# Gate and value products of six token tiles as seven block products, in an attention and expert kernel on one Trainium2 core

## The chip, the core and the metric

The kernel runs on one core of one Trainium2 chip. A core has a matrix engine (TensorE, "PE" in the profile, with its weight loads shown apart as "PEld"), and three engines for elementwise work: VectorE ("DVE"), ScalarE ("ACT") and GpSimd ("POOL"). SyncE ("SP") issues most transfers between DRAM and the core's memory SBUF. TensorE writes its sums to PSUM, which has eight banks of 512 fp32 values for each of 128 partitions; DVE and ACT read them there, POOL does not. Each engine works through its own queue in order; waits between engines are semaphores.

The metric is the time on the device in microseconds, the median of several runs. Where a profile is read, it is that of one execution.

## What is computed

Attention over a sliding window of 64 positions, then a normalised gated expert layer on its output:

```python
scores = q @ k.T / sqrt(64), masked to 0 <= i - j < 64        # 8 batches, 8 heads, 576 positions, 64 wide
attn   = softmax(scores) @ v                                  # -> x: 4608 tokens x 512
xn     = x / sqrt(mean(x * x) + 1e-6) * rms_g
g      = xn @ w_gate                                          # 512 x 1536
val    = xn @ w_val                                           # 512 x 1536
out    = (g * sigmoid(g) * val) @ w_out                       # 1536 x 512
```

Inputs and output are fp32. The kernel gets fp32 accuracy out of fp16 matmuls: each operand is split into a high and a low fp16 part, and a product is the sum of three matmuls (high x high, high x low, low x high), all into the same PSUM bank.

## The kernel before

**Tiles and chunks.** The 4608 tokens are worked off in nine tiles of 512 tokens (`t`, 0 to 8). The 1536 hidden columns are six chunks of 256 (`c`, 0 to 5). For a tile, `expert_in(t, c)` (L821) goes over the two halves `i` of a chunk (128 columns) and makes a gate group (`pg`) and a value group (`pv`): 4 slices of the 512 inputs by three matmuls, each 128x128 weights against 512 tokens. A group fills one of three rotating PSUM banks (`ps_mo`). ACT takes the tanh of the gate (L838), DVE makes the silu of it and multiplies by the value (L839, L840), ACT rounds the result to fp16 (L841), and POOL, or DVE in the last chunk, subtracts to get the low part (L842). The hidden values of a chunk stay in `hs[t, c]`, out of six buffers. After the six chunks, `expert_out(t)` (L1018) multiplies by `w_out`: four blocks `k` of 128 tokens by 12 halves of chunks by three matmuls of 512 columns (`po`), then a scaled copy on ACT (L1003) and a store by SP.

**Attention between them.** Attention for batches 2 to 7 is spread over tiles 0 to 6 as "visits" (L618), one per pair of heads. A visit has the scores of pair `n` on TensorE (L386), masks on DVE (L399) and exponentials on ACT (L402), and the values product of pair `n - 2` (L507). Between the two, POOL scales and moves the weights in 16 small instructions (`move`, L371) and DVE transposes them (`turn`, L374). Then come root mean squares (`roots_of_all`, L697) and `normalise` (L726), which scales `x` and splits it into `xn`. A batch has 576 tokens, so one of its two pieces belongs to one tile and the other to the next.

**Order.** A counter of half steps drives all this. `tick()` (L797) advances it, and everything in `plan` that is due is traced: 32 half steps for a tile, 24 in `expert_in` and 8 in `expert_out`. A planner then orders the instructions of each engine by priority (order of writing) and by modelled readiness. From tile 1, chunk 3, on (`ORDERED`), `group()` (L83) pins TensorE's instructions to the written order; the other engines stay with the planner.

**Code that does not run.** `prepare` (L856), `load_sevens`, `product`, `operands`, `combine` and `expert_in_7` (L933) build a tile from seven block products. They apply to tiles from `FIRST7` on, and `FIRST7 = NT` (9), so no tile uses them here.

**Buffers the change touches.** `wt[0..11]` hold gate and value weights (high and low) of the six chunks, `wt[12..17]` those of `w_out`, `wt[18]` and `wt[19]` are spare. `t2k` is a ring of eight buffers of 2 KB per partition, used for tanh results, stores, roots and sums.

## Time and profile before

| | |
|---|---|
| median of 3 runs | 1028.23 us (1027.82 to 1029.15) |
| the profiled execution, first to last instruction | 1027.3 us |
| mean granted TensorE clock | 0.988 |
| data moved by DMA | 66.11 MB |
| tile 1, about | 208 to 321 us |
| tiles 3, 4, 5, 6, about | 421, 525, 629, 733 us to the next |
| tiles 7 and 8 (without visits), about | 837 to 930.6 and 930.6 to 1024 us |

The profile was taken in one execution; its span leaves out what lies around the first and the last instruction, and the median of the runs is 0.9 us above it. The page gives each engine's busy time and its share of the span, then the costliest groups of instructions by line. Views of the trace give the same for any stretch, the waits of one engine for another, and the instructions in order of time. A group's line names the source line, engine, operation, output and inputs with shapes and count, then busy time and the mean in ns of one instruction, then idle time before it and what ended that. Matmuls are pipelined, so the duration of one (0.38 us for 512 columns) is longer than the distance from one start to the next.

### The profile page before, as it was taken

How to read it: one execution, taken by the hardware profiler on the slowest of the kernel's cores; microseconds unless marked ns; L12 is line 12 of the kernel's file. 1: busy time of each engine (PE TensorE's matmuls, PEld its weight loads, DVE VectorE, ACT ScalarE, POOL GpSimd, SP SyncE). 2: the span in 40 equal slices, each digit the busy share in tenths (PEclk: the TensorE clock that was granted, in tenths of full speed). 3: DMA queues.
4: the chain of work that ended last, by engine and by line, in shares of the span. 5: the costliest groups of instructions: out<-in, count | busy, mean ns of one | idle time of the engine just before them, and what ended most of it. 6: DMA issues, size and time to landing. Idle time of an engine off the chain costs nothing.

```text
span 1027.3 us, 16840 instructions
## 1 busy us (share of the span) xinstructions
PE 993.8 (97%) x6455; PEld 497.1 (48%) x6455; DVE 480.2 (47%) x1333; ACT 409.8 (40%) x1066; POOL 483.6 (47%) x634
## 2 busy tenths in 40 slices
PE   7789989999999999999999999999999999999998
PEld 5544544554444445444544454445444444444445
DVE  5688966343474348333843384337532432201220
ACT  5558885254333433344334433343442222212220
POOL 3326633467856576557645764576455022101200
PEclk9989989999999999999999999999999999999999
DMA  8535641221112111211121112111100000000001
GB/s 288 194 108 178 209 150 47 78 69 45 49 57 78 47 48 67 68 47 47 60 75 48 47 57 78 47 48 45 66 2 1 11 31 1 1 23 20 1 1 41
DMA packets 27793, 66.11 MB, mean 64 GB/s; under 512 B 3008, under 2 KB 3264, under 8 KB 27712
## 3 DMA queue, kind: packets, MB, share of 16 engines
q1 hardware_dynamic: 27136, 63.85, 19.1%
q8 instruction: 51, 0.84, 0.3%
q10 hardware_dynamic: 576, 1.18, 0.3%
q14 instruction: 30, 0.25, 0.1%
HBM read 55.58 MB, written 9.44 MB: 63 GB/s over the span
## 4 chain that ended last, share of the span: by engine, by line
PE 89%; ACT 3%; POOL 2%; DVE 2%; DMA 1%; issue 1%; SPq 0%; ACTq 0%; POOLq 0%; DVEq 0%
PE po L790 9%; PE po L791 9%; PE po L792 9%; PE pv L790 9%; PE pv L791 8%; PE pv L792 8%; PE pg L790 8%; PE pg L791 8%; PE pg L792 8%; PE sc L386 4%; PE xp L507 2%; POOL pm L371 2%; PE x L507 2%; PE tr L489 1%; DMA kv<-kv 1%
## 5 line engine op out<-in xcount | busy, mean ns | idle before, releaser
L371 POOL TENSOR_TENSOR pm<-pm,st 32x288 f32<-32x288 f32 (+1 forms) x384 | 252.8, 658 | 117.9 <-DVE st L428 38.9
L842 POOL TENSOR_TENSOR h<-th,h 128x512 f16<-128x512 f32 x90 | 105.5, 1177 | 184.6 <-ACT h L841 176.3
L790 PE MATMUL pv<-xn,wt 128*128 128x512 f16 x432 | 165.1, 382 | 4.4 <-DVE th L839 4.4
L839 DVE SCALAR_TENSOR_TENSOR th<-th,pg 128x512 f32<-128x512 f32 x108 | 73.7, 683 | 203.8 <-ACT th L838 203.6
L790 PE MATMUL pg<-xn,wt 128*128 128x512 f16 x432 | 163.8, 379 | 1.7 <-ACT wt L235 1.7
L791 PE MATMUL pv<-xn,wt 128*128 128x512 f16 x432 | 165.0, 382 | 0.0
L792 PE MATMUL pv<-xn,wt 128*128 128x512 f16 x432 | 164.8, 381 | 0.0
L791 PE MATMUL pg<-xn,wt 128*128 128x512 f16 x432 | 163.9, 379 | 0.0
L792 PE MATMUL pg<-xn,wt 128*128 128x512 f16 x432 | 163.8, 379 | 0.0
L790 PE MATMUL po<-wt,h 128*128 128x512 f16 (+1 forms) x436 | 162.8, 373 | 0.0
L791 PE MATMUL po<-wt,h 128*128 128x512 f16 (+1 forms) x436 | 162.7, 373 | 0.0
L792 PE MATMUL po<-wt,h 128*128 128x512 f16 (+1 forms) x436 | 162.7, 373 | 0.0
L841 ACT CAST h<-th 128x512 f16<-128x512 f32 x105 | 64.8, 617 | 227.5 <-DVE th L840 227.5
L791 PEld LDWEIGHTS <-wt 128*128 128x128 f16 x872 | 85.6, 98 | 104.8 <-issue 6.5
L792 PEld LDWEIGHTS <-wt 128*128 128x128 f16 x872 | 85.6, 98 | 103.3 <-issue 1.7
L790 PEld LDWEIGHTS <-wt 128*128 128x128 f16 x872 | 85.5, 98 | 103.4 <-issue 2.5
L838 ACT ACTIVATE th<-pg,hsc 128x512 f32<-128x512 f32 x108 | 74.0, 686 | 101.4 <-PE pg L792 85.3
L840 DVE SCALAR_TENSOR_TENSOR th<-pv,th 128x512 f32<-128x512 f32 x108 | 74.0, 685 | 71.3 <-PE pv L792 70.7
L402 ACT ACTIVATE pm<-pm,st 128x128 f32<-128x128 f32 (+1 forms) x216 | 83.3, 387 | 32.6 <-DVE st L399 32.4
L748 POOL TENSOR_TENSOR xn<-xb,xn 128x64 f16<-128x64 f32 (+7 forms) x63 | 49.1, 806 | 83.4 <-ACT xn L746 83.0
L1003 ACT ACTIVATE ot<-po,hsc 128x512 f32<-128x512 f32 (+1 forms) x37 | 25.0, 674 | 120.7 <-PE po L792 120.4
L790 PEld LDWEIGHTS <-h 128*128 128x128 f16 x436 | 42.8, 98 | 48.2 <-issue 0.8
(144 smaller groups left out, 1091.8 us busy)
## 6 DMA issues: line engine op xcount, KB each, us to landing
kv<-kv SPq DMA_DIRECT2D x28, 608.0 KB, 4.5
out<-ot SPq DMA_DIRECT2D x35, 256.0 KB, 2.0
q<-q SPq DMA_DIRECT2D x28, 288.0 KB, 2.8
kv<-kv SPq DMA_DIRECT2D x56, 128.0 KB, 4.6
st<-w_gate SPq DMA_DIRECT2D x6, 1024.0 KB, 5.7
st<-w_val SPq DMA_DIRECT2D x6, 1024.0 KB, 5.8
st_o<-w_out SPq DMA_DIRECT2D x6, 1024.0 KB, 5.0
kv<-kv SPq DMA_DIRECT2D x4, 320.0 KB, 6.2
```

Source lines behind the costliest of these rows:

```text
L371: nc.gpsimd.tensor_tensor(m[to, :us, fr], p[fr, :us, to], r, ALU.mult)
L386: nc.tensor.matmul(out.rearrange("p (n c) -> p n c", c=D), lhsT=qt[hd, j * D : (j + 1) * D], rhs=halves[hd, :1, :] if j == 0 else halves[h ...
L402: nc.scalar.activation(part, part, AF.Exp, bias=low, scale=-1.0, accum_out=total)
L748: eng.tensor_tensor(xn[:, 1, kt, o : o + n], x, hi, ALU.subtract)
L790: nc.tensor.matmul(acc, lhsT=lh, rhs=rh, start=first, stop=False)
L791: nc.tensor.matmul(acc, lhsT=lh, rhs=rl, start=False, stop=False)
L792: nc.tensor.matmul(acc, lhsT=ll, rhs=rh, start=False, stop=last)
L838: nc.scalar.activation(th, acc[0], AF.Tanh, scale=th_scale[:, c : c + 1])
L839: nc.vector.scalar_tensor_tensor(th, th, 1.0, acc[0], ALU.add, ALU.mult)
L840: nc.vector.scalar_tensor_tensor(th, acc[1], 2.0**-41, th, ALU.mult, ALU.mult)
L841: (nc.vector.tensor_copy if t < 2 and E('HHE', 'a' * 24)[12 * t + f] == 'v' else nc.scalar.copy)(hh, th)
L842: (nc.vector if t and c == NC - 1 else nc.gpsimd).tensor_tensor(hl, th, hh, ALU.subtract)
```

## The change

Tiles 3 to 8 compute gate and value of a chunk by seven products of blocks half the size. Take the chunk's 512 inputs as two halves, and the tile's 512 tokens as two halves. Combinations of weight blocks and of token blocks are formed once; seven block products and a few sums of them give what eight give directly (a form of Strassen's scheme). Here a weight block is half of the inputs (two slices of 128) by half of the chunk (128 hidden columns), and a token block is half of the inputs by 256 tokens. One product makes gate and value (`i` = 0 and 1, the two halves of one PSUM bank), each by two slices and three matmuls of 128x128 weights against 256 tokens: 12 matmuls.

What it does, part by part:

- **`FIRST7 = 3`.** Tiles 0 to 2 go as before; tiles 3 to 8 go through `all_sevens`.
- **`prepare(c, i)`**, 12 calls, due at half steps 34 to 72 (tile 1 and the start of tile 2; step 32 begins tile 1). Each copies plain blocks of the weights to DRAM by four transfers, adds high and low parts to fp32 on DVE, makes four sums of blocks on DVE, splits them again (two copies on ACT, one subtraction on POOL and one on DVE) and stores two tiles of 256 KB to DRAM.
- **`load_sevens`** reads 1792 KB for each chunk of each such tile from DRAM into four of the twelve weight buffers, three chunks in turn. The first three are asked for in tile 2; each later one after product 4 of the chunk three before.
- **`combine`** replaces the splitting of `xn` for these tiles: per piece of a batch four sums on DVE and seven pairs of copy (ACT) and subtraction (POOL), where there were four pairs.
- **`seventh(t, c, p)`** runs product `p` into a PSUM bank. Products 1, 5 and 6 are copied to SBUF by ACT (`snap`); products 2, 3 and 7 have a copy added by DVE; the products 6, 7, 4 go on in the bank of 1, and 3 in that of 5. `quad` makes a quarter of the chunk's hidden values: tanh of 256 columns on ACT and two steps of 256 columns on DVE.
- **One pool of PSUM banks.** From tile 3 on the seven pools are closed and a single pool of eight banks serves products, visits, roots and outputs.
- **Written order.** `all_sevens` lays a tile out in 66 slots. Product `p` of chunk `c` stands at slot `7c + PLACE[p]`; free slots from 42 on take the output product, one (block, chunk) pair of six matmuls each, and its last two run over into slots 1 and 5 of the next tile. The half steps that drive the visits are spread evenly over the slots.

```diff
-FIRST7 = NT
+FIRST7 = 3
+SLOTS = 66
+PLACE = {1: 0, 5: 2, 2: 3, 6: 4, 3: 6, 7: 8, 4: 12}
-PREP0, PREP1 = 32.2, 55.5
+PREP0, PREP1 = 34.0, 72.0
+    def prepare(c, i):
+        w = wt[2 * c + i].rearrange("p a (k f) -> p a k f", k=NKD)
...
+        for j in range(2):
+            part = out_of[:, at + TT * j : at + TT * (j + 1)].rearrange("p (k f) -> p k f", k=NKD)
+            nc.sync.dma_start(out=part, in_=w[:, j, :, :P])
+            part = out_of[:, at + 2 * TT + HT * j : at + 2 * TT + HT * (j + 1)].rearrange("p (k f) -> p k f", k=2)
+            nc.sync.dma_start(out=part, in_=w[:, j, 2:, P:])
...
+        for d in range(2):
+            rd = r[d].rearrange("p (k f) -> p k f", k=2)
+            nc.vector.tensor_tensor(rd, w[:, 0, 2 * d : 2 * d + 2], w[:, 1, 2 * d : 2 * d + 2], ALU.add)
...
+        nc.vector.scalar_tensor_tensor(a22, a21, -1.0, a22, ALU.mult, ALU.subtract)
+        nc.vector.tensor_tensor(a21, a11, a21, ALU.subtract)
+        nc.vector.tensor_tensor(a11, a11, a22, ALU.add)
+        nc.vector.tensor_tensor(a12, a12, a11, ALU.add)
...
+            nc.scalar.copy(h, src)
+            (nc.vector if d else nc.gpsimd).tensor_tensor(l, src, h, ALU.subtract)
+        for j, x in enumerate((hi, lo)):
+            nc.sync.dma_start(out=out_of[:, 2 * TT * (2 * i + j) : 2 * TT * (2 * i + j + 1)], in_=x)
...
+    def seventh(t, c, p):
+        if p in (1, 2, 5):
+            acc = any_bank(f"a{p}_{t}_{c}")
+        else:
+            acc = kept[c, "w" if p == 3 else "x"]
+        with group():
+            product(t, c, p, acc, p in (1, 2, 5))
+        if p == 1:
+            kept[c, "x"] = acc
+            snap(acc, t, c, 1)
+        elif p == 5:
+            kept[c, "w"] = acc
+            snap(acc, t, c, 5)
+        elif p == 6:
+            snap(acc, t, c, 6)
+        elif p == 2:
+            nc.vector.tensor_tensor(acc, acc, kept.pop((c, 1)), ALU.add)
+            quad(t, c, 0, 0, acc)
+        elif p == 3:
+            nc.vector.tensor_tensor(acc, acc, kept.pop((c, 6)), ALU.add)
+            quad(t, c, 0, 1, acc)
+        elif p == 7:
+            p5 = kept.pop((c, 5))
+            nc.vector.tensor_tensor(p5, acc, p5, ALU.add)
+            quad(t, c, 1, 1, p5)
+        else:
+            quad(t, c, 1, 0, acc)
+            load_sevens(NC * (t - FIRST7) + c + 3)
...
+    for n in range(2 * NC):
+        at_step(PREP0 + (PREP1 - PREP0) * n / (2 * NC), partial(prepare, n // 2, n % 2))
...
+    early.close()
+    shared["banks"] = ctx.enter_context(tc.tile_pool(name="ps_8", bufs=8, space=PSUM))
+    late = ctx.enter_context(tc.tile_pool(name="late", bufs=1))
+    all_sevens()
```

More of the change, by code (lines that the diff above doesn't have):

```diff
@@ L407, in scores_of_pair @@
         sc = [
-            pool.tile([P, TT], F32, tag=tag, name=f"sc_{n}_{h}").rearrange("p (i k) -> p i k", k=P)
+            (any_bank(f"sc_{n}_{h}") if shared else pool.tile([P, TT], F32, tag=tag, name=f"sc_{n}_{h}"))
+            .rearrange("p (i k) -> p i k", k=P)
             for h, (pool, tag) in enumerate(((ps_sc, "sc"), (ps_tr, "tr")))
@@ L898, in load_sevens, with block @@
+    def block(p, i, j):
+        if p in SUMS:
+            return 2 * TT * (2 * i + j) + HT * SUMS[p]
+        at = 8 * TT + 3 * TT * i
+        return at + (2 * TT + HT * j if p == 4 else TT * j + HT * (p - 1))
+    SUMS = {6: 0, 7: 1, 3: 2, 5: 3}
     def load_sevens(r):
@@ new lines, in tile_window_attention_moe, with snap, quad @@
+    kept = {}
+    def snap(src, t, c, p):
+        d = wt[11][:, 1, :].bitcast(F32) if p == 5 else late.tile([P, TT], F32, tag=f"s{p}", name=f"s{p}_{t}_{c}")
+        nc.scalar.copy(d, src)
+        kept[c, p] = d
+    def quad(t, c, i, half, acc):
+        if (c, "th", i) not in kept:
+            kept[c, "th", i] = wk.tile([P, TT], F32, tag="t2k", name=f"th_{t}_{c}_{i}", bufs=T2K), []
+        th, done = kept[c, "th", i]
+        cols = th[:, half * HT : (half + 1) * HT]
+        nc.scalar.activation(cols, acc[:, :HT], AF.Tanh, scale=th_scale[:, c : c + 1])
+        nc.vector.scalar_tensor_tensor(cols, cols, 1.0, acc[:, :HT], ALU.add, ALU.mult)
+        nc.vector.scalar_tensor_tensor(cols, acc[:, HT:], 2.0**-41, cols, ALU.mult, ALU.mult)
+        done.append(half)
+        if len(done) == 2:
+            kept.pop((c, "th", i))
+            hh, hl = hs[t, c][:, 0, i, :], hs[t, c][:, 1, i, :]
+            nc.scalar.copy(hh, th)
+            (nc.vector if c == NC - 1 else nc.gpsimd).tensor_tensor(hl, th, hh, ALU.subtract)
@@ new lines, in all_sevens, with out_unit @@
+    def all_sevens():
+        units = {}
+        outs = []
+        for t in range(FIRST7, NT):
+            base = SLOTS * (t - FIRST7)
+            for c in range(NC):
+                for p, at in PLACE.items():
+                    units[base + (NC + 1) * c + at] = partial(seventh, t, c, p)
+            last = NC - 1
+            order = [(0, c) for c in range(last)] + [(1, c) for c in range(last - 1)] + [(0, last), (1, last - 1), (1, last)]
+            order += [(k, c) for k in range(2, TT // P) for c in range(NC)]
+            outs += [(base + (NC + 1) * last + 7, t, k, c) for k, c in order]
+        pos = {}
+        def out_unit(t, k, c):
+            if t == NT - 1 and k == TT // P - 1:
+                if c == 0:
+                    for e in range(2):
+                        es = slice(e * DM // 2, (e + 1) * DM // 2)
+                        po = any_bank(f"po_{t}_{k}_{e}")[:, es]
+                        for c in range(NC):
+                            chunk_out(po, t, c, k, c == 0, c == NC - 1, es)
+                        store(po, t, k, es)
+                return
+            if c == 0:
+                pos[t, k] = any_bank(f"po_{t}_{k}")
+            po = pos[t, k]
+            chunk_out(po, t, c, k, c == 0, c == NC - 1)
+            if c == NC - 1:
+                store(po, t, k)
+        n = SLOTS * (NT - FIRST7)
+        for slot in range(n):
+            h = half_steps * (FIRST7 - 1) + half_steps * slot / SLOTS
+            while steps["now"] <= half_steps + h:
+                tick()
+            if slot in units:
+                units.pop(slot)()
+            elif outs and slot >= outs[0][0]:
+                out_unit(*outs.pop(0)[1:])
+        assert not units
+        while outs:
+            out_unit(*outs.pop(0)[1:])
@@ L1022, in expert_out @@
                 es = slice(e * DM // halves, (e + 1) * DM // halves)
[L1023 removed]
+                po = ps_mo.tile([P, DM], F32, tag="mo", name=f"po_{t}_{k}_{e}")[:, es]
                 for c in range(NC):
@@ L1119, in tile_window_attention_moe @@
             first_full = 2
[L1120 to L1134 removed]
+    for t in range(first_full, FIRST7):
+        for c in range(NC):
+            in_order["on"] |= (t, c) >= ORDERED
+            expert_in(t, c)
+            if t == FIRST7 - 1 and c % 2:
+                load_sevens(c // 2)
         expert_out(t)
+    early.close()
+    shared["banks"] = ctx.enter_context(tc.tile_pool(name="ps_8", bufs=8, space=PSUM))
+    late = ctx.enter_context(tc.tile_pool(name="late", bufs=1))
+    all_sevens()
     assert not plan
[L1137 removed]
 def kernel(**inputs):
```

150 lines of the change are left out of this document (25 added, 125 removed).

## The prediction

> **What bounds the kernel now.** I read the page first, then a view of busy time by stretches cut at the tile borders, then TensorE's own waits, then the last 25 us instruction by instruction.
>
> ```profile
> span 1027.3 us, 16840 instructions
> PE 993.8 (97%) x6455; PEld 497.1 (48%) x6455; DVE 480.2 (47%) x1333; ACT 409.8 (40%) x1066; POOL 483.6 (47%) x634
> ```
>
> The columns of the second view are length, then busy time and instructions of each engine (PEld is the weight load, beside PE), granted clock and DMA.
>
> ```profile
> core 0: us, PE busy (x) PEld busy (x) DVE busy (x) ACT busy (x) POOL busy (x), PEclk, DMA share, GB/s
> 208.00:321.00 113.00, 108.46 (x829) 54.50 (x828) 58.48 (x188) 48.13 (x162) 75.97 (x104) 1.00 0.20 61
> 421.00:525.00 104.00, 104.00 (x734) 51.51 (x730) 51.18 (x148) 40.57 (x120) 62.91 (x84) 1.00 0.19 56
> 837.00:930.60 93.60, 93.60 (x436) 42.42 (x434) 17.95 (x26) 18.41 (x28) 11.55 (x10) 1.00 0.03 12
> ```
>
> The rows are tile 1, tile 3 and tile 7. In the last two TensorE is busy for the whole stretch at a granted clock of 1.00, and no other engine is busy for two thirds of it. Only tile 1 has holes, 113.0 - 108.5 = 4.5 us. So from tile 2 on the time is the number of matmuls times their pitch, and what leaves TensorE's queue leaves the span, as long as no other engine turns late. A busy TensorE is not one at its peak, so I need the pitch:
>
> ```profile
> 999.66 0.38 PE L790 MATMUL po<-wt,h 128*128 128x512 f16 x1
> ...
> 1015.64 0.38 PE L792 MATMUL po<-wt,h 128*128 128x512 f16 x1
> 1015.85 0.27 PE L790 MATMUL po<-wt,h 128*128 128x256 f16 x1
> 1015.85 0.10 PEld L791 LDWEIGHTS <-h 128*128 128x128 f16 x1
> ...
> 1019.78 0.27 PE L790 MATMUL po<-wt,h 128*128 128x256 f16 x1
> ...
> 1023.60 0.27 PE L792 MATMUL po<-wt,h 128*128 128x256 f16 x1
> ```
>
> 75 matmuls of 512 columns start 15.98 us apart from first to last: 15.98 / 74 = 0.216 us each. Then come 72 of 256 columns, the shape the change uses: 7.75 / 71 = 0.1092 us each, a new weight load with every one. The load (0.10) fits under a 256-column matmul with a hundredth of a microsecond to spare. Tile 7 confirms the pitch: 432 x 0.216 = 93.3 of its 93.6 us.
>
> **The term that goes.** One 256-column chunk of gate and value takes 4 groups x 12 = 48 matmuls of 512 columns now, 10.37 us. After, it is 7 products x 12 = 84 matmuls of 256 columns, 9.17 us. Saved: 1.20 us, times 6 chunks and 6 tiles, **43.1 us**. The output product and the attention stay. A tile with attention would go from 104.0 to 96.8 us.
>
> The code for block products in the kernel before never runs (its first tile is NT), so nothing else is removed. The 252 products each begin with a wait on another engine. At 1019.78 the second half of the columns starts in a new accumulator, and the pitch holds. If each product's start laid one weight load bare, it would cost 252 x 0.10 = 25 us. I take nothing, the nearest row, and keep 25 as the far end.
>
> The Trainium skill's page "TensorE: Matmul & The Clock Gate" (Part 3, The mechanism) speaks against this change: it says that a weight load overlaps running matmuls only when they use different row groups, and here all use the whole array. By that rule every load would be paid beside its matmul. The rows above disagree, 0.1092 us for both together; the price is a rival below.
>
> **What the vector engines get, per chunk.** Rows by shape, mean ns of one:
>
> ```profile
> L838 ACT ACTIVATE th<-pg,hsc 128x512 f32<-128x512 f32 x108 | 74.0, 686 | 101.4 <-PE pg L792 85.3 <-POOL h L842 15.7
> L839 DVE SCALAR_TENSOR_TENSOR th<-th,pg 128x512 f32<-128x512 f32 x108 | 73.7, 683 | 203.8 <-ACT th L838 203.6
> L841 ACT CAST h<-th 128x512 f16<-128x512 f32 x105 | 64.8, 617 | 227.5 <-DVE th L840 227.5
> L842 POOL TENSOR_TENSOR h<-th,h 128x512 f16<-128x512 f32 x90 | 105.5, 1177 | 184.6 <-ACT h L841 176.3 <-DVE h L841 6.0
> L842 DVE TENSOR_TENSOR h<-th,h 128x512 f16<-128x512 f32 x16 | 13.2, 828 | 7.5 <-ACT h L841 7.5
> L492 DVE COPY pt<-tr 128x256 f32<-128x256 f32 x16 | 6.7, 418 | 6.7 <-PE tr L489 6.6
> L694 DVE SCALAR_TENSOR_TENSOR r<-r,r 128x256 f32<-128x256 f32 x6 | 3.5, 582 | 0.2
> L1003 ACT ACTIVATE ot<-po,hsc 128x256 f32<-128x256 f32 x2 | 0.9, 473 | 6.7 <-PE po L792 6.7
> L748 POOL TENSOR_TENSOR xn<-xb,xn 128x256 f16<-128x256 f32 x8 | 5.7, 738 | 5.4 <-ACT xn L746 5.3
> ```
>
> DVE now does 4 x 0.683 = 2.7 us. After: 3 sums with PSUM (512 columns, 0.68 each) and 8 steps of 256 columns, which lie between 0.418 (a 256 copy out of PSUM) and 0.683; I take 0.45: 2.1 + 3.6 = 5.7. ACT: 3 snapshots (nearest 0.617), 4 tanh of 256 (0.473) for 2 of 512 (0.686): 2.4 more. Per tile DVE gets 6 x 3.0 = 18 and ACT 14. The operand sums per batch add some 8 DVE instructions and six more copy-and-subtract pairs on ACT and POOL: 8 x 0.58, 6 x 0.47 and 6 x 0.74, so 5, 3 and 4 us. A tile with attention then has DVE 51 + 18 + 5 = 74, ACT 58 and POOL 67 of 96.8 us. No engine passes TensorE; DVE, at 76%, comes nearest.
>
> **Their slack decides.** Products 1 and 6 share a bank with three products between them: 3 x 12 x 0.1092 = 3.9 us, in which the snapshot (0.6) must be through. The same holds from 6 to 7, from 7's sum to 4, and from 5 to 3. Now three banks rotate, two groups ahead are 5.2 us, tanh and multiply take 1.4: 3.8 left. So 3.3 remain where 3.8 did, with more work ahead in each queue. Elsewhere there is room: product code holds at most four of the eight banks and a visit four; chunk 5's last hidden values take 0.5 + 2 x 0.45 + 0.6 + 0.8 = 2.8 us, and the output product wants them five slots of 1.3 later; the next tile's first operand needs some 9 roots' steps and 4 scalings (13 x 0.58) and a pair (1.2), 9 us, in the 15 slots left at step 25, 20 us.
>
> ```profile
> 523.43 0.27 PE L386 MATMUL x<-kv,q 64*64 64x64 f32 x2
> ...
> 525.76 0.39 PE L790 MATMUL po<-wt,h 128*128 128x512 f16 x1
> 524.08 0.35 ACT L402 ACTIVATE pm<-pm,st 128x64 f32<-128x64 f32 x1 [2.81 <-DVE st L399]
> ...
> 528.71 0.68 ACT L570 ACTIVATE ssq<-xb 128x576 f32<-128x576 f32 x1
> DVE pm L374 <- POOL pm L371: 63.1, 20, 5.4
> ```
>
> An attention visit keeps ACT for 5.3 us (524.08 to 529.39), of which the first 1.7 lie beside its own 2.3 us on TensorE, so a snapshot may come 3 us late: just inside. Worse is DVE standing before the transpose (L374) for POOL's moves: 3.2 us on average, 5.4 at most, and the sums, tanh and snapshots queue behind it. The mean is all of the slack, the longest exceeds it by 2. With 16 visits in tiles 3 to 6 that is 0 to 32 us; I take **4**, since the mean just fits.
>
> **The weight sums (prepare).** Twelve halves at steps 34, 37.2, ... 68.8; ten fall in tile 1 (steps 32 to 63). Each: on DVE two adds and a subtract of 512 columns (0.828) and four sums of 256 (0.582), 4.8 us; on ACT two copies, 1.2; on POOL one subtract, 1.2; on SP six transfers, the last two behind those subtracts. Tile 1 gets DVE 58 + 48 = 106 of 113 us, POOL 76 + 12. It is also the one place where TensorE already waits:
>
> ```profile
> PE pv L790 <- DVE th L839: 1.6, 1, 1.6
> PE x L386 <- DMA kv<-kv: 1.5, 1, 1.5
> PE x L507 <- DVE st L399: 1.4, 1, 1.4
> ```
>
> A half that runs on DVE in one piece (4.8) exceeds the slack of 3.8 by 1.0, twelve times 12 us; broken up by other work it costs nothing. I take **5** and keep 0 to 25, as each half also pushes POOL's moves, behind which values and loads wait.
>
> Two-input DVE work beside POOL is slower, and the sums are of that kind:
>
> ```profile
> 307.47 0.95 DVE L693 TENSOR_TENSOR r<-r 128x192 f32<-128x192 f32 x1
> 310.42 0.36 DVE L693 TENSOR_TENSOR r<-r 128x192 f32<-128x192 f32 x1
> 305.64 4.53 POOL L748 TENSOR_TENSOR xn<-xb,xn 128x384 f16<-128x384 f32 x4 [3.12 <-ACT xn L746]
> ```
>
> The same instruction takes 0.95 while POOL is busy (to 310.17) and 0.36 after. The Trainium skill's page "SBUF — State Buffer" (SBUF: two separate sides) gives the reason as an exclusive lock on a port pair that the two share, held for a whole instruction; the trace agrees. If all seven DVE instructions of a half lost the 0.6 us that these rows show, ten halves would lay 42 us more on DVE in tile 1, about 148 of 113: the heavy rival below.
>
> **New loads.** Each chunk of a product tile reads 1792 KB from DRAM, into buffers free after product 4 of three chunks back: eight products later it is needed, 10.5 us, plus 2.3 if a visit lies between.
>
> ```profile
> kv<-kv SPq DMA_DIRECT2D x28, 608.0 KB, 4.5
> st<-w_gate SPq DMA_DIRECT2D x6, 1024.0 KB, 5.7
> SPq L336 <- POOL ssq L575: 68.2, 13, 11.8
> ```
>
> From 608 KB in 4.5 us to 1024 KB in 5.7 is 1.2 us for 416 KB, so 1792 KB should land in about 7.9 us: hidden by 2.6. Only three chunks of a tile (18 loads) are that tight, the others have the output product between. The pool change at tile 3 I put at **1** (a store's copy and its wait); the tail is the same.
>
> **The sum.** 1027.3 - 43.1 + 4 + 5 + 1 = 994.2 for the profiled span; the median of the runs lies 0.9 above it: **995**.
>
> **Rivals.**
> - *All hidden.* Only the 43.1 counts: 1028.2 - 43 = 985. For: tiles 2 to 8 show no wait now, and the load on each engine stays under 80%. Against: DVE's wait before L374 is as long as the slack. 0.16.
> - *DVE falls behind.* Halves run in one piece or meet POOL (12 to 25 us), and each of 16 visits shows 1 us: 985 + 13 + 16 = 1014; with the port loss in full 1026. For: DVE at 94% in tile 1. Against: no sum has to be early, the last is read in tile 3. 0.24.
> - *Loads late* (the slow side). SP issues in order. The wait of a kv load for POOL's ssq, 68.2 / 13 = 5.2 us, may stand ahead of the weights. If so for all 18, each is late by 7.9 + 5.2 - 10.5 = 2.6 us, 47 us in sum, and with the 10 of the main case 1042. It decides from 1.8 us a load (33 us over 18). Against: kv loads come just after visits, and two of a tile's three tight loads are issued before one. 0.06.
> - *The loads of weights aren't covered*, so the change doesn't save: 84 x (0.109 + 0.10) = 17.6 against 48 x (0.216 + 0.10) = 15.2 per chunk, 36 x 2.4 = 86 us more: 1114. The tail speaks against it. This is the rule of the TensorE page named above. 0.01.
>
> **How the numbers follow.** Main case 988 to 1004 with 0.51; 985 with 0.16; 1004 to 1026 with 0.24; the rest, 0.09, near or above 1028. This kernel's measurement tells about 0.2% (2 us) from no change. Faster 0.91, same 0.02, slower 0.07. The range runs from 985 to 1019: it leaves out the top of the DVE case, the slow ones and the lowest corner.
>
> **What would show it.** In the changed profile: products starting every 0.109 us; tiles 7 and 8 at 86 to 87 us and tiles 3 to 6 at 97 to 99; a tile 1 of 113 to 120 us, with waits of TensorE on DVE; TensorE's waits in tiles 3 to 6 on the snapshots and the sum of product 7, next to visits. The prediction is wrong if the pitch in the products is over 0.115, if products wait on DMA, if tile 1 grows by over 15 us, or if tiles 7 and 8, which have no attention, exceed 90.

## The result, and the profile after

The changed kernel takes 1045.59 us (median of 4 runs, 1044.15 to 1047.58) against 1028.03 us (1027.75 to 1029.15) for the kernel before on the same chip: ratio 1.0168, 95% interval 1.0152 to 1.0184. It is 1.7% slower, where I had put 995 us. (Of the runs below, one of the six executions of e15b took 4795.1 us and is left out of its median.)

```profile
span 1045.8 us, 20545 instructions
...
PE 975.9 (93%) x7751; PEld 632.9 (61%) x7751; DVE 668.9 (64%) x1713; ACT 510.6 (49%) x1303; POOL 543.1 (52%) x679
...
PE 58%; DVE 18%; POOL 12%; ACT 7%; issue 3%; DMA 2%; SPq 0%; POOLq 0%; DVEq 0%; ACTq 0%
```

The last line is from the chain of work that ended last. DVE and POOL hold 30% of it now, 4% in the kernel before; no engine but TensorE looks full, and TensorE itself is down to 93%. The view by stretches, with the columns of the prediction, cut where the first gate matmul or product of tiles 1, 2, 4 and 7 starts:

```profile
211.00:348.20 137.20, 116.52 (x797) 57.02 (x797) 110.84 (x262) 59.37 (x181) 101.67 (x116) 0.93 0.27 90
348.20:459.00 110.80, 106.29 (x725) 52.39 (x724) 66.64 (x165) 44.87 (x131) 74.38 (x95) 0.98 0.37 115
...
561.50:667.80 106.30, 100.87 (x941) 74.33 (x940) 72.96 (x196) 55.22 (x157) 68.43 (x91) 0.97 0.51 162
...
866.90:953.00 86.10, 86.10 (x649) 63.42 (x648) 37.58 (x71) 34.55 (x62) 18.83 (x16) 1.00 0.44 144
```

Tile 7 is where I had put it, and full. Tile 1 is 25 us longer than before, tile 2 7 us, and tile 4, which should be at 97, is at 106. The products themselves, in the order of time (start, duration; a row of "x12" is one product):

```profile
879.98 1.47 PE L922 MATMUL a<-xn,wt 128*128 128x256 f16 x12
881.29 1.47 PE L922 MATMUL a<-wt,wt 128*128 128x256 f16 x12
882.60 4.09 PE L922 MATMUL a<-xn,wt 128*128 128x256 f16 x36
886.53 2.78 PE L922 MATMUL a<-wt,wt 128*128 128x256 f16 x24
889.15 1.04 PE L922 MATMUL a<-xn,wt 128*128 128x256 f16 x8
```

84 matmuls from 879.98 to 889.15: 9.17 us, the chunk I had worked out. So the saving is there, and what eats it is in the waits (us in total, times, longest):

```profile
DVE pm L377 <- POOL pm L374: 48.1, 19, 5.2
...
PE x L511 <- DVE st L402: 34.7, 13, 6.9
...
PE pv L794 <- DVE th L843: 8.9, 5, 3.9
```

L402 is the mask of a visit, L511 its values product. They meet in a bank: the scores of a pair's first block stand in the bank that the values of the pair two visits earlier are written to. The end of tile 3, TensorE and then DVE:

```profile
553.09 0.38 PE L796 MATMUL po<-wt,h 128*128 128x512 f16 x1
557.51 1.53 PE L511 MATMUL x<-pm,kv 64*64 64x64 f32 x20 [4.04 <-DVE st L402]
558.98 0.61 PE L794 MATMUL po<-wt,h 128*128 128x512 f16 x1
...
561.51 0.85 PE L922 MATMUL a<-xn,wt 128*128 128x256 f16 x3
```

```profile
534.27 0.42 DVE L692 TENSOR_SCALAR r<-tot 128x256 f32<-128x256 f32 x1 [0.96 <-PE tot L704]
...
542.58 2.99 DVE L744 SCALAR_TENSOR_TENSOR xb<-xb,gsb,r 128x256 f32<-128x256 f32 x4
545.50 1.23 DVE L377 STREAM_TRANSPOSE pm<-pm 128x1024 f32<-128x1024 f32 x1
...
549.40 0.48 DVE L692 TENSOR_SCALAR r<-tot 128x320 f32<-128x320 f32 x1
...
555.38 1.94 DVE L744 SCALAR_TENSOR_TENSOR xb<-xb,gsb,r 128x320 f32<-128x320 f32 x4
557.23 0.22 DVE L402 CUSTOM_DVE_ANT_0 pm<-x,blocked 128x64 f32<-128x64 f32 x1
```

From 534.3 DVE works without a hole: roots and scaling of one piece, the transpose, the token sums of that piece, then roots and scaling of the second piece (its token sums follow the mask). The mask of the visit, whose scores were done by 551.4, comes at 557.2. After the wait the clock is half: six output matmuls start 2.53 / 6 = 0.42 us apart (558.98 to 561.51), not 0.216. In the kernel before, at the same place of tile 4:

```profile
603.53 0.36 DVE L688 TENSOR_SCALAR r<-tot 128x192 f32<-128x192 f32 x1 [1.14 <-PE tot L700]
...
621.39 2.87 DVE L740 SCALAR_TENSOR_TENSOR xb<-xb,gsb,r 128x384 f32<-128x384 f32 x4
627.75 0.23 DVE L399 CUSTOM_DVE_ANT_0 pm<-x,blocked 128x64 f32<-128x64 f32 x1 [3.50 <-PE x L386]
```

The same unbroken run, 21 us, and then DVE waited 3.5 us for the scores. That was its whole slack. The change takes 9 us from the interval (the last two visits of a tile are 24 us apart, 33 before, since slots share out the half steps evenly) and puts the token sums of the first piece into the run. Between the visit at 526.1 and the next visit's mask at 557.2 DVE is busy for 26.9 us, more than the whole interval.

In tile 1, DVE and then TensorE:

```profile
293.99 1.25 DVE L377 STREAM_TRANSPOSE pm<-pm 128x1024 f32<-128x1024 f32 x1 [5.20 <-POOL pm L374]
...
297.88 1.28 DVE L870 TENSOR_TENSOR r<-wt 128x512 f32<-128x512 f16 x2
299.09 0.21 DVE L402 CUSTOM_DVE_ANT_0 pm<-x,blocked 128x64 f32<-128x64 f32 x1
```

```profile
299.36 1.53 PE L511 MATMUL x<-pm,kv 64*64 64x64 f32 x20 [6.87 <-DVE st L402]
```

DVE stands (waits at the head of its queue) for 5.2 us before the transpose for POOL's moves, then does what has piled up, weight sums (L870) among it, and the mask is 6.9 us late.

### The profile page after: what moved, and what is told of

Its sections match the earlier page's. It is cut to its first block, busy times and chain, and to the rows that moved or that the text cites. A ratio compares the mean times of both kernels' runs of the same rounds, so it can differ in the third digit from the quotient of the medians.

```text
span 1045.8 us, 20545 instructions
## 1 busy us (share of the span) xinstructions
PE 975.9 (93%) x7751; PEld 632.9 (61%) x7751; DVE 668.9 (64%) x1713; ACT 510.6 (49%) x1303; POOL 543.1 (52%) x679
## 4 chain that ended last, share of the span: by engine, by line
PE 58%; DVE 18%; POOL 12%; ACT 7%; issue 3%; DMA 2%; SPq 0%; POOLq 0%; DVEq 0%; ACTq 0%
PE a L922 26%; POOL pm L374 10%; PE po L794 6%; PE po L795 6%; PE po L796 6%; DVE xb L744 3%; PE sc L389 2%; ACT pm L405 2%; DVE r L697 2%; DVE r L698 2%; PE xp L511 2%; DVE r L699 2%; PE x L511 2%; DVE pm L377 1%; PE pv L794 1%
## 5 line engine op out<-in xcount | busy, mean ns | idle before, releaser
L922 PEld LDWEIGHTS <-wt 128*128 128x128 f16 x3024 | 295.8, 98 | 42.9 <-issue 2.2
L922 PE MATMUL a<-xn,wt 128*128 128x256 f16 x1728 | 203.8, 274 | 1.2 <-ACT ot L1041 0.8
L954 POOL TENSOR_TENSOR h<-th,h 128x512 f16<-128x512 f32 x60 | 69.1, 1159 | 154.5 <-ACT h L953 139.3
L922 PE MATMUL a<-wt,wt 128*128 128x256 f16 x1224 | 146.2, 273 | 0.0
L947 DVE SCALAR_TENSOR_TENSOR th<-th,a 128x256 f32<-128x256 f32 x108 | 45.3, 419 | 65.1 <-ACT th L946 65.0
L946 ACT ACTIVATE th<-a,hsc 128x256 f32<-128x256 f32 x108 | 51.3, 475 | 52.6 <-PE a L922 29.8
L796 PEld LDWEIGHTS <-h 128*128 128x128 f16 x436 | 43.1, 99 | 49.4 <-issue 2.2
L794 PEld LDWEIGHTS <-h 128*128 128x128 f16 x436 | 43.3, 99 | 46.9 <-issue 3.0
L795 PEld LDWEIGHTS <-h 128*128 128x128 f16 x436 | 43.1, 99 | 46.0 <-issue 3.4
L794 PE MATMUL pv<-xn,wt 128*128 128x512 f16 x144 | 57.6, 400 | 8.9 <-DVE th L843 8.9
L389 PE MATMUL sc<-kv,q 64*64 64x128 f32 (+1 forms) x1056 | 56.5, 296 | 8.1 <-DMA q<-q 5.1
L777 ACT CAST xn<-xb 128x192 f16<-128x192 f32 (+7 forms) x33 | 12.9, 423 | 101.7 <-DVE xb L744 101.5
L377 DVE STREAM_TRANSPOSE pm<-pm 128x1024 f32<-128x1024 f32 x24 | 29.8, 1243 | 48.1 <-POOL pm L374 48.1
L511 PE MATMUL x<-pm,kv 128*64 128x64 f32 (+1 forms) x480 | 26.1, 250 | 34.7 <-DVE st L402 34.7
```

The source lines that it names most:

```text
L389: nc.tensor.matmul(out.rearrange("p (n c) -> p n c", c=D), lhsT=qt[hd, j * D : (j + 1) * D], rhs=halves[hd, :1, :] if j == 0 else halves[h ...
L511: nc.tensor.matmul(xp[hd, c * D : (c + 1) * D], lhsT=vv[j][rows, hd], rhs=w, start=True, stop=True, skip_group_check=True,)
L794: nc.tensor.matmul(acc, lhsT=lh, rhs=rh, start=first, stop=False)
L795: nc.tensor.matmul(acc, lhsT=lh, rhs=rl, start=False, stop=False)
L796: nc.tensor.matmul(acc, lhsT=ll, rhs=rh, start=False, stop=last)
L922: nc.tensor.matmul(acc[:, i * HT : (i + 1) * HT], lhsT=ws[l][:, kt, :], rhs=b[:, m, kt, :], start=at_start, stop=kt == 1 and j == 2, skip_ ...
```

## The experiments

Theory: the loss is (a) the weight sums in tiles 1 and 2 and (b) the end of tiles 3 to 5, both through DVE's order. Rivals: the transfers, the products' own evacuation, the pool of banks. The table has all runs: median, ratio to the kernel before on the same chip with its interval, and the lengths of tiles 1 to 7 from the trace (first gate matmul or product of a tile to that of the next).

| run | us | ratio | t1 | t2 | t3 | t4 | t5 | t6 | t7 |
|---|---|---|---|---|---|---|---|---|---|
| before | 1028 | 1 | 112.5 | 103.9 | 103.9 | 103.9 | 103.9 | 99.6 | 93.2 |
| after | 1045.6 | 1.0168 | 137.2 | 110.8 | 102.5 | 106.3 | 105.7 | 93.4 | 86.1 |
| e1 | 1052.8 | 1.0233 (1.0218-1.0248) | 133.9 | 106.3 | 103.9 | 103.9 | 103.9 | 99.6 | 93.2 |
| e2 | 1030.4 | 1.0017 (1.0008-1.0026) | 111.9 | 107.6 | 103.8 | 107.2 | 106.5 | 92.9 | 86.1 |
| e3 | 1043.2 | 1.0141 (1.0124-1.0158) | 136.7 | 110.8 | 95.7 | 105.4 | 104.9 | 99.7 | 86.1 |
| e4 | 1055.2 | 1.0257 (1.0241-1.0272) | 136.3 | 110.4 | 106.6 | 109.2 | 109.2 | 92.9 | 86.1 |
| e5 | 1039.9 | 1.0110 (1.0095-1.0125) | 136.7 | 107.5 | 103.2 | 105.0 | 105.4 | 92.9 | 86.1 |
| e6 | 1045.8 | 1.0163 (1.0148-1.0178) | 130.2 | 117.1 | 102.3 | 106.5 | 106.0 | 92.9 | 86.1 |
| e7_from6 | 1037.6 | 1.0080 (1.0065-1.0095) | 114.3 | 109.4 | 108.2 | 111.8 | 112.6 | 90.3 | 86.1 |
| e7_from7 | 1041.8 | 1.0126 (1.0109-1.0143) | 112.6 | 111.4 | 106.1 | 107.3 | 115.4 | 100.6 | 83.5 |
| e8 | 1033.3 | 1.0046 (1.0031-1.0061) | 114.1 | 107.3 | 108.9 | 109.1 | 114.2 | 90.3 | 86.1 |
| e9 | 1052.4 | 1.0224 (1.0209-1.0240) | 143.8 | 109.2 | 107.3 | 100.9 | 103.0 | 97.1 | 86.1 |
| e9_from6 | 1039.2 | 1.0098 (1.0082-1.0115) | 114.1 | 109.0 | 107.3 | 109.0 | 109.9 | 100.1 | 86.1 |
| e10 | 1044.3 | 1.0144 (1.0122-1.0166) | 138.9 | 107.0 | 103.6 | 105.8 | 106.1 | 92.9 | 86.1 |
| e11 | 1007.4 | 0.9787 (0.9771-0.9803) | 107.5 | 103.9 | 103.9 | 103.9 | 106.9 | 90.3 | 86.1 |
| e12 | 1052.0 | 1.0230 (1.0212-1.0247) | 134.4 | 103.9 | 103.9 | 103.9 | 103.9 | 99.6 | 93.2 |
| e13 | 1023.0 | 0.9952 (0.9934-0.9970) | 107.5 | 103.9 | 103.9 | 103.9 | 103.9 | 99.6 | 93.2 |
| e14 | 1003.7 | 0.9762 (0.9742-0.9782) | 108.0 | 103.9 | 103.9 | 104.9 | 99.5 | 92.5 | 86.1 |
| e15b | 1023.6 | 0.9953 (0.9932-0.9973) | 107.3 | 108.6 | 103.5 | 105.8 | 106.1 | 92.9 | 86.1 |
| e15 | 1001.9 | 0.9745 (0.9725-0.9764) | 107.3 | 104.9 | 101.5 | 97.6 | 98.5 | 92.5 | 86.1 |

**e1, sums alone.**

```diff
-FIRST7 = 3
+FIRST7 = NT
```

> All nine tiles as in the kernel before; the twelve halves of weight sums are made and stored, and never read. Theory (the sums are what tile 1 and tile 2 lose, +24.7 and +6.9 us in the changed kernel): 1028 + 31 = about 1059 us, tile 1 near 137 us, tiles 3 to 8 as before. Rival (the sums alone cost what I predicted, 5 us, and tile 1 grew for another reason, for instance the planner's order of what comes later): 1033 us, tile 1 below 120.

24 us, in tile 1 (21.4) and tile 2 (2.4) alone: the theory's side, 7 us short of its 31. Tiles 1 and 3:

```profile
209.80:343.70 133.90, 113.05 (x797) 55.96 (x797) 106.55 (x257) 58.46 (x178) 98.60 (x112) 0.96 0.28 94
...
450.00:554.00 104.00, 104.00 (x726) 51.47 (x725) 51.11 (x145) 40.58 (x120) 62.97 (x85) 1.00 0.19 57
```

**e2, the sums' arithmetic left out.**

```diff
-        r = [wk.tile(...) for d in range(2)]
...
+        for j in range(2):
+            nc.sync.dma_start(out=out_of[:, 2 * TT * (2 * i + j) : 2 * TT * (2 * i + j + 1)], in_=wt[2 * c + i][:, j, :])
```

> The changed kernel without the arithmetic of the weight sums: the transfers that fill the DRAM copy stay, plain weights stand where the sums would be (the output is another). Theory (DVE, ACT and POOL work of the sums holds tile 1 and 2): about 1045.6 - 31 = 1015 us, tile 1 back at 113 and tile 2 at 104, tiles 3 to 5 still at 105. Rival (the transfers and SP's queue do it): above 1035 us, tile 1 still above 130.

Tiles 1 and 2 together are 28.5 us shorter (248.0 to 219.5), so arithmetic and not transfers. The total falls by only 15 us, mostly since tile 0 took 160.4 us and not 151.6: in all three runs without the sums it was 8 to 11 us longer, with a wait of 5 to 6 us of TensorE for a `kv` transfer that the others lack. SP issues that transfer at about the same time (163.6 in e2, 162.3 in the changed kernel), but in e2 the scores that wait for it stand ahead of a value group in TensorE's queue. Why the order differs there isn't known, so those runs are read by tiles. Tile 2 stays 3.7 us longer than before even without the sums, with a wait of 2.5 us for the mask of its last visit.

**e3, a bank of its own for the first block.**

```diff
-            visits[n][0](xp[:, XSPLIT:])
+            visits[n][0](any_bank(f"fi_{n}") if shared else xp[:, XSPLIT:])
```

> The changed kernel, and from tile 3 on the 64 scores of a pair's first block get a PSUM bank of their own, so that the values product of the pair two visits earlier does not share it with them and does not wait for their mask. Theory (the shared bank lays DVE's backlog bare): the waits of 1.2 to 4.7 us at the visits of tiles 3 to 6 go, 18 us, and 5 us of lowered clock behind them: 1045.6 - 23 = about 1023 us. Rival (DVE is late anyway, and what comes next on TensorE, the second half of the values or a product whose bank waits for DVE's sum, waits in its place): within 5 us of 1045.6.

The rival: the values no longer wait, and TensorE does three products later, 3.42 us for a snapshot (L937) that ACT makes behind the exponentials of the late mask. The wait now falls into the next tile (t3 less, t6 more; tiles 3 to 6 sum to 405.7 against 407.9). DVE is late; the bank only says where it shows.

**e4, the old share of the half steps.**

```diff
-            h = half_steps * (FIRST7 - 1) + half_steps * slot / SLOTS
+            tile_no, s = divmod(slot, SLOTS)
+            h = half_steps * (FIRST7 - 1 + tile_no) + (24 * s / 45 if s < 45 else 24 + 8 * (s - 45) / 21)
```

> The changed kernel with the half steps of a tile laid over its 66 slots as they lay in time before: 24 half steps on the first 45 slots, the last 8 on 21 slots (before this run, 8 half steps on 16.5). Normalising, and with it roots, scaling and the sums of token blocks, gets 31 us up to the last visit, as in the kernel before, and not 24. Theory (DVE has too little time at the end of a tile): the waits of 4.0 to 4.7 us at the ends of tiles 3 to 5 go, 13 us and 4 of clock: about 1029 us. Rival (the visits, now 22 us apart in the first part of a tile in place of 24, make DVE wait longer for POOL's moves before the transpose): 1045 us or slower.

Slower, against the theory as I put it. The last visit's scores start at 549.85, 31 us after the visit before:

```profile
551.04 1.94 DVE L744 SCALAR_TENSOR_TENSOR xb<-xb,gsb,r 128x320 f32<-128x320 f32 x4
553.01 0.96 DVE L783 TENSOR_TENSOR t<-xb 128x320 f32<-128x320 f32 x1
...
556.07 0.89 DVE L789 TENSOR_TENSOR t<-xb,t 128x320 f32<-128x320 f32 x1
556.89 0.21 DVE L402 CUSTOM_DVE_ANT_0 pm<-x,blocked 128x64 f32<-128x64 f32 x1
```

The planner set the mask behind the token sums (553.0 to 557.0), and the run had begun 10 us after the visit, not 8. Length of the interval is not the only thing; the order in it counts.

**e5, token sums left out.**

```diff
-        nc.vector.tensor_tensor(t3, x22, x12, ALU.subtract)
...
+        parts("t1", x12)
+        parts("t2", x22)
+        parts("t3", x12)
+        parts("t4", x21)
```

> The changed kernel without the four sums of token blocks on DVE per piece of a batch: the seven pairs of copy and subtraction stay, and work on plain blocks (the output is another). The run e4 gave the last visit of a tile 31 us in place of 24, and its mask still came 7 us late, because the planner had put the four sums ahead of it. Theory (roots, scaling and token sums are one unbroken run of 28 us on DVE, and the mask of the visit stands behind it): 6.4 us less per tile on DVE, so the waits of 4.0 to 4.7 us at the ends of tiles 3 to 5 go, with the lowered clock behind them: tiles 3 to 5 near 98 us, in all about 1027 us. Rival (roots beside POOL's moves are what is too long, 0.75 us where 0.42 would do; the sums only add to it): waits shrink by less than half, 1038 us or more.

The rival: tiles 3 to 5 gained 1 us in all. Roots, scaling and the transpose alone run from 529.0 to 550.3 and overrun a visit at 545.0.

**e6, e7, where the halves stand.**

```diff
-PREP0, PREP1 = 34.0, 72.0
+PREP0, PREP1 = 34.0, 87.0        # e6
+PREP0, PREP1 = 66.0, 183.0       # e7_from6, with FIRST7 = 6
+PREP0, PREP1 = 66.0, 215.0       # e7_from7, with FIRST7 = 7
```

> The changed kernel with the twelve halves of weight sums at half steps 34 to 82.6 in place of 34 to 68.8: seven of them in tile 1 and five in tile 2, where ten and two were. Theory (tile 1 loses because DVE is overfull there, so the loss falls faster than the number of halves): tile 1 near 124 us and tile 2 near 110, in all about 1033 us. Rival (each half costs about 2.5 us wherever it stands): tile 1 near 130, tile 2 near 118, in all about 1045 us.

> Products only in tiles 6, 7 and 8, and the twelve halves of weight sums spread from half step 66 to 173 (tiles 2 to 5, one in 9.75 half steps). Theory (the products gain what was predicted where DVE has room; the sums cost little where DVE is half idle and each has its own 30 us): tile 6 near 93, tiles 7 and 8 near 86 and 89, no wait of over 1 us in tiles 2 to 5: 1028 - 6 - 7 - 4.5 - 0 to + 3 = 1010 to 1014 us. Rival (each half costs 2 to 2.5 us wherever it stands, as it did in the run of sums alone): 1010 + 24 to 30 = 1034 to 1040 us.

> Products only in tiles 7 and 8, which have no attention visits, and the halves of weight sums spread from half step 66 to 203 (tiles 2 to 6, one in 12.4 half steps). Theory: tiles 7 and 8 near 86 and 89 us, nothing else changes: 1028 - 7 - 4.5 + 0 to 3 = 1016 to 1020 us, some 6 us above the kernel with products from tile 6. Rival (each half costs 2 us or more everywhere): 1040 us or more.

Rival in all three. In e6 tile 1 gives 7.0 us and tile 2 takes 6.3: some 2 us a half. In e7 even one half in 40 us lays a wait open, mostly of the values for the mask, and most where it falls between the last two visits (tile 5 of e7_from7: 6.6 us). My picture of a queue that is overfull only in tile 1 fell here.

**e8, halves right behind a visit.**

```diff
-        at_step(PREP0 + (PREP1 - PREP0) * n / (2 * NC), partial(prepare, n // 2, n % 2))
+        at_step(half_steps * (2 + n // 3) + (3.5, 11.5, 19.5)[n % 3], partial(prepare, n // 2, n % 2))
```

> As the kernel with products from tile 6, but each of the twelve halves of weight sums stands 4 half steps after a visit (phases 3.5, 11.5 and 19.5 of tiles 2 to 5), where the halves of the two kernels before laid no gap open; none stands between the last two visits of a tile. Theory (a half costs only where DVE or POOL has less slack to the next visit's mask than the half takes: DVE idles 3.5 us ahead of the last visit of a tile in the kernel before, and POOL's moves leave little in the others): gaps of TensorE in tiles 2 to 5 fall from 24 to under 8 us: 1037.5 - 15 to - 22 = 1016 to 1022 us. Rival (each half costs some 2 us wherever it stands, through POOL's subtraction and the slower DVE beside it): 1032 to 1038 us.

Rival by its time, but now each tile from 2 to 5 shows the same: no wait at its first visit, 0.2 us at the second, 2.7 at the third (0.45 and 3.0 when counted from the start of the last score matmul, as below). POOL's ten moves there in e8, and in the kernel before:

```profile
480.91 8.82 POOL L374 TENSOR_TENSOR pm<-pm,st 32x288 f32<-32x288 f32 x10
```

```profile
474.64 7.05 POOL L371 TENSOR_TENSOR pm<-pm,st 32x288 f32<-32x288 f32 x10
```

And what DVE and TensorE of e8 make of it:

```profile
495.04 1.25 DVE L377 STREAM_TRANSPOSE pm<-pm 128x1024 f32<-128x1024 f32 x1 [5.78 <-POOL pm L374]
```

```profile
499.22 1.39 PE L511 MATMUL x<-pm,kv 64*64 64x64 f32 x20 [2.74 <-DVE st L402]
```

DVE's part of the half was through at 488. But DVE's sums slow POOL's moves beside them, 0.88 us each in place of 0.71, DVE stands for them 5.8 us, and behind the transpose queue gate work and then the mask. In the kernel before the transpose was as close: it started at 463.86 after a stand of 3.74, DVE was free at 466.5, and the values came at 468.0, so with 0.2 for the mask some 1.3 us were left. And it isn't needed then: the order of DVE's instructions has the transpose of pair n, which the visit of pair n + 2 uses, ahead of the mask of pair n + 1. The planner sets it a whole visit early, where it has to stand.

**e9, the second piece after the last visit.**

```diff
-        events = ... + [(n0, partial(normal, 0)), (n1, partial(normal, 1))]
+        events = ... + [(n0, partial(normal, 0))]
+        if FIRST7 <= b < B - 1:
+            events += [(n1, defer)] + [(LATER + 0.8 * k, resume) for k in range(6)]
...
+    x5 = cp.tile([P, 5, S], F32, name="xb")
-... T2K ... = ... 8 ...
+... T2K ... = ... 7 ...
```

> The changed kernel, and at the ends of tiles 3, 4 and 5 the second piece of the batch (needed only a whole tile later) is normalised after the last visit, in five steps from half step 1 to 4.2 of the next tile; only its sum of squares and the first instruction of its roots stay ahead. The five pairs' worth of x stand in one buffer of five slots, so that the next batch's first pair does not overwrite it, and the ring of 2 KB buffers is 7 instead of 8 to make room. Theory (the last visit's mask comes late because 28 us of DVE work stand in 24 us between two visits, 11 of them for this piece): the waits of 4.2 to 4.7 us at the ends of tiles 3 to 5 go, with the lowered clock behind them, tiles 3 to 5 at 97 to 100 us: about 1022 to 1028 us. Rival (the work is late wherever it stands: the next tile's first products, or the mask of its first visit, wait instead): tiles 3 to 5 at 103 us or more, 1040 us or more.

> Both edits together: products from tile 6, halves of weight sums 4 half steps after a visit in tiles 2 to 5, and the second piece of the batch at the end of tile 5 normalised after the last visit. Theory: the wait at the end of tile 5 (4.3 us and the clock behind it, 8 us in all in the kernel with products from tile 6) goes too: 4 to 8 us below the kernel with the phases alone, about 1012 us. Rival: no difference to it within 2 us.

Rival again in the first: the waits at the ends of tiles 3 to 5 shrink to 2 us or nothing, but others come, such as the next tile's second chunk for a snapshot:

```profile
482.97 5.28 PE L959 MATMUL a<-xn,wt 128*128 128x256 f16 x24 [3.62 <-ACT wt L974]
```

Tile 1 also lost 6.6 us, with a wait of 11.0 us for a `kv` transfer. The second, e9_from6, fits neither side: it is 5.8 us slower than e8, since tile 5 gains 4.3 us and tile 6 loses 9.8, with a wait of 4.8 us for a snapshot.

**e10 to e12, the transpose at its written place.**

```diff
-MOVES = (8.7, 7, 4.5, 4)
+MOVES = (4, 7, 4.5, 4)
...
-                events.append((visit_at(n + 2) - half_steps * (b - 1) - 3, partial(turned, hp)))
+                at_visit = visit_at(n + 2) - half_steps * (b - 1)
+                lead = 7.2 if at_visit % half_steps == 31.5 else 3
+                events.append((at_visit - lead, partial(behind, [partial(turned, hp)], (nc.vector,))))
```

> The changed kernel, and the transpose of a pair's weights on DVE is kept at its written place (after all DVE work written before it; 3 half steps ahead of the visit that needs it, 7.2 where that visit is the last of a tile). In the kernels so far the planner sets it one whole visit earlier, where DVE stands 3.7 us (before) to 5.8 us (e8) for POOL's moves, with the next visit's mask and the sums queued behind; after the transpose only some 1.3 us were left to the mask in the kernel before. The moves of a batch's first pair are due at 4 half steps after its visit in place of 8.7. Theory (that stand is what turns any DVE work beside POOL's moves into a wait of TensorE): tile 1 near 125 us (137), tile 2 near 106 (111), the mid-tile waits of tiles 3 to 5 go and those at their ends shrink by the 1.5 us of the transpose: about 1020 to 1028 us. Rival (DVE is overfull in tile 1 and at tile ends, whatever the order): above 1040 us.

> The kernel with products from tile 6 and the halves 4 half steps after a visit (1033.3 us), with the transposes at their written place as in the run above. There every tile from 2 to 5 had the same two waits, 0.45 us at its second visit and 3.0 us at its third, each with DVE standing 5.6 to 5.8 us for POOL's moves, which took 0.88 us each in place of 0.71 beside the sums. Theory (the stand, not the sums' own time): these waits go, tiles 2 to 5 back to 104 to 105 us: about 1015 us. Rival (a half costs TensorE time through DVE's own 7 us in the visit's interval): 1030 us or more.

> All nine tiles as in the kernel before, the twelve halves of sums made and never read, as in the run that priced them at 24 us, and the transposes at their written place. Theory (half or more of the price of the sums is the stand before the transpose): 1028 + 8 to 12 = about 1038 us, tile 1 near 122 us in place of 134. Rival (DVE's own load in tile 1): 1048 us or more.

e11 takes the theory's side, and by more than expected: 1007.4 us, 26 us under e8 by this edit (the transposes' place and the first pair's earlier moves together; no run separates them). All twelve halves are still there (DVE has 70 us in tile 2, 51 in the kernel before), and tiles 1, 2, 4 and 5:

```profile
211.50:319.00 107.50, 107.50 (x797) 53.88 (x797) 59.53 (x186) 47.36 (x157) 74.75 (x101) 1.00 0.22 67
319.00:423.00 104.00, 104.00 (x726) 51.47 (x725) 69.88 (x167) 43.53 (x126) 72.76 (x88) 1.00 0.23 72
...
526.90:630.80 103.90, 103.90 (x725) 51.41 (x724) 73.24 (x171) 44.77 (x129) 74.58 (x91) 1.00 0.23 73
630.80:737.70 106.90, 104.38 (x725) 51.36 (x724) 75.19 (x174) 46.00 (x133) 76.98 (x95) 1.00 0.37 117
```

What went is the stand, not the slowness of the moves. DVE's waits before the transpose in e8, and ten moves of POOL in e11, where no wait before a transpose is left:

```profile
DVE pm L377 <- POOL pm L374: 82.1, 19, 6.0
```

```profile
448.77 8.83 POOL L374 TENSOR_TENSOR pm<-pm,st 32x288 f32<-32x288 f32 x10
```

e10 and e12 take the rival's. Their mid-tile waits in tiles 2 to 5 are gone (tile 2 of e12: 103.9, 106.3 in e1), but tile 1 stays at 139 and 134, with other names in TensorE's waits there (e10):

```profile
PE x L511 <- DVE st L402: 7.6, 2, 6.6
PE x L389 <- DMA kv<-kv: 7.1, 2, 6.9
PE pv L796 <- DVE th L845: 5.4, 2, 4.6
```

At the ends of tiles 3 to 5 of e10 the waits grew, against the theory: 5.4, 4.7 and 5.5 us in place of 4.0, 4.3 and 4.5. So two things were at work: ten halves in tile 1, whose first visits are only 5 half steps apart, are too many in both orders tried; in tiles 2 to 4, back at 103.9 in e11, it was the stand (tile 5 keeps 3.0 us, which no run separates). One part of tile 1 can be read from e12: its longest wait, 8.3 us, is for a `kv` transfer that SP issued at 264.74, when POOL's sum of squares ended, and that stood behind twelve moves of POOL that took 10.48 us. In e13 below, without sums, the same transfer was issued at 247.22.

**e13, that order in the kernel before.** `FIRST7 = NT`, no weight sums, the edit of e10.

> The kernel before (no products, no sums) with the transposes at their written place, to price that edit by itself beside the 1007 us of e11. Theory (TensorE had no room to gain but in tile 1, where it waited 4.5 us): tile 1 near 107.5 in place of 112.5, all else unchanged: 1023 us; so of e11's 21 us some 5 are the order and 16 the products of tiles 6 to 8. Rival (the order alone is the gain): below 1015 us.

As expected: 5 us, all in tile 1. So some 17 of e11's 22 us are the products of tiles 6 to 8, less what their sums still cost.

**e15b and e15, the end of a tile.** The edits of e2 and e10; e15 adds that of e9, with `LATER = 33.6` and steps of 0.85.

> The changed kernel without the arithmetic of the weight sums (plain weights stand in their place, the output is another) and with the transposes at their written place: the products from tile 3, free of tile 1's load and of the stand before the transpose. What is left is the end of a tile. Theory: tile 1 near 107.5, tile 2 near 104, tiles 3 to 5 at 102 to 106 with one wait of 4.5 to 5.6 us each at the last visit: about 1008 us. Rival (the sums hid something else in the products): tiles 3 to 5 still show other waits, 1015 us or more.

> As the run before it (no weight sums, transposes at their written place), and the second piece of a batch normalised after the last visit, in five steps from half step 1.6 to 5 of the next tile (ring of 2 KB buffers 7 in place of 8). Theory (the end of a tile loses because 28 us of DVE work stand in 24 us between two visits): the three waits go and nothing takes their place: tiles 3 to 5 near 97, 24 us less than the run without this edit, about 985 us, which is what I had predicted as the case with all hidden. Rival (the DVE work is late wherever it stands, as in e9, where the next tile's products then waited): less than 8 us below the run without it.

Tiles 4 and 5 of e15b and then of e15:

```profile
540.50:646.30 105.80, 101.05 (x942) 74.31 (x941) 76.43 (x195) 54.84 (x156) 68.70 (x90) 0.97 0.50 161
646.30:752.40 106.10, 100.54 (x941) 74.08 (x940) 76.34 (x195) 55.15 (x157) 68.56 (x91) 0.97 0.48 154
```

```profile
531.90:629.50 97.60, 97.51 (x941) 72.65 (x940) 71.11 (x191) 52.54 (x148) 67.20 (x90) 1.00 0.52 169
629.50:728.00 98.50, 98.33 (x941) 72.88 (x940) 73.94 (x195) 53.89 (x155) 66.82 (x90) 1.00 0.51 167
```

e15b has one wait at the end of each of tiles 3 to 5 (5.4, 4.7 and 5.5 us), as its theory had it, though its total is on the rival's side. e15 takes the theory's: 21.7 us between the two, and tiles 4 and 5 are full at 97.6 and 98.5, the 97 to 99 that I had predicted for them. Tile 3 stays at 101.5, with a wait of 1.8 us for a mask and shorter ones. With the transposes out of the way the late piece finds room, which it did not in e9. The totals lie 16 and 17 us over their expectation, 8 to 11 of it in tile 0 as in e2.

**e14, a whole kernel from tile 5.** The edits of e10 and e15, `FIRST7 = 5`, and:

```diff
-        at_step(PREP0 + (PREP1 - PREP0) * n / (2 * NC), partial(prepare, n // 2, n % 2))
+    for n, h in enumerate((35, 45, 51.5, 67.5, 75.5, 83.5, 99.5, 107.5, 115.5, 131.5, 139.5, 147.5)):
+        at_step(h, partial(prepare, n // 2, n % 2))
```

> A whole kernel again: products from tile 5, nine halves of the weight sums 4 half steps after visits of tiles 2 to 4 and three in tile 1, transposes at their written place, and the second piece of a batch (ends of tiles 5 and 6) normalised after the last visit. Theory: tile 5 at 97 in place of 107, tile 6 without the wait at its start, the three halves in tile 1 cost up to 5 us: 998 to 1004 us, 3 to 9 below e11. Rival (the late piece makes tile 6's products wait, or the halves in tile 1 cost 3 us each): 1008 us or more.

1003.7 us, within the theory's range: 2.4% under the kernel before and 4% under the change as made. Tile 5 is at 99.5, not 97, with a wait of 1.9 us for a snapshot. Its interval overlaps that of e11, so which of these two is faster is not settled. Three halves in tile 1 cost 0.5 us there.

## Why the prediction was wrong

**The term that goes: right.** 9.17 us a chunk, 86.1 us for tile 7. No product waited for a transfer, and no weight load was laid bare: the rivals "loads late" and "weights not covered" did not happen. The pool change cost one wait of 0.8 us, as put.

**The weight sums (5, at most 25): the first wrong step.** Tiles 1 and 2 grew by 24.7 + 6.9 = 31.6 us; the sums alone cost 24 (e1). I set the length of one half (4.8) against the slack of the gate groups' banks (3.8), and put a half that is broken up at nothing. DVE's load was as I had worked it out (106.6 us in tile 1 of e1, 106 predicted); what failed is that the slack of the banks was to decide. Of the waits of TensorE in tile 1, 14.5 us were those of a visit's values for its mask and 6.1 those of gate groups. In tile 3 of the kernel before, the mask had some 1.3 us, because it stood behind a transpose that stood for POOL. I had quoted that stand (63.1 us in 20) and charged it to the steady tiles only, as a fixed time; I had taken the lock between DVE and POOL as a loss for DVE, and not as one for POOL's moves, for which DVE then stands. For tiles 2 to 4 this is shown, since without the stand their halves cost nothing (e11, and tile 2 of e12). For tile 1, where most of the loss lies, it isn't: there the same edit saved nothing (134.4 us in e12, 133.9 in e1), and all that is shown is that the sums' arithmetic does it (e1, e2).

**The steady stalls (4, at most 32): the second.** From tile 3's first matmul to the last of all the change gained 15.0 us (597.7 to 582.7), not 43.1 - 5 = 38.1. Snapshots and the sum of product 7, for which I worked out 3.3 us of slack, are not what waited in the changed kernel, but for one wait of 0.4 us. The failing step is "the next tile's first operand needs some 9 roots' steps and 4 scalings (13 x 0.58) and a pair (1.2), 9 us, in the 15 slots left at step 25, 20 us": I followed the operand of the first piece and not DVE's queue up to the next fixed point. Roots and scaling of the first piece alone took 11.3 us (534.3 to 545.6), since roots beside POOL's moves take 0.70 to 0.78 us each, not 0.58. With the token sums, the transpose and the second piece the run is 23 us long ahead of a mask, and it begins 8 us into an interval that the even slots cut from 33 to 24 us. e5 shows that the token sums alone don't decide it, e4 that a longer interval alone doesn't mend it. e15b against e15 shows the price: 21.7 us.

These two, 26.6 and 23.1 us over what I had put, with 2 us at the start and the end, are the 52 us between 994.2 and 1045.8. The rival "DVE falls behind" had the right engine and ended at 1026, with neither mechanism sized. Some 4 of the 26.6 belong to the second step, since tile 2 is 3.7 us longer even without sums (e2). What stays open: which of DVE's work, POOL's moves or the `kv` loads holds tile 1 with ten halves in it, since e10 only changed which of them is named; and the order in tile 0 of the runs without sums.

## What to carry to other kernels

Set an engine's work against the interval between two points that can't move (here two visits), all of it that is queued ahead of the second point, and not against the mean of a tile: at 49% of a tile DVE had 3.5 us left at its end. When an instruction stands for another engine, ask whether its result is due yet; moving a transpose to where it was written, with one pair's moves earlier, made the nine blocks of added work in tiles 2 to 4 free in e11. And a change that evens out a schedule also shortens the intervals that used to be long.
